# Reading wo inside the attention passes in 8 to 16 KB runs, with a selection product that permutes o and dO

## The chip, the cores and the metric

One core of one Trainium2 chip. The metric is the device time of one execution in microseconds. Runs of one kernel in one job lie 4 to 14 us apart (0.2 to 0.7%), which is as large as the effect that was looked for, so each comparison below is of runs on the same chip in the same job. A ratio is the mean time of one kernel's fast runs over the mean of the other's fast runs of the same rounds, so it is not quite the ratio of the medians that stand beside it. Microseconds given for a ratio are (ratio - 1) x 2029, the median of the kernel before in the first of those jobs.

## The reference, cut to what matters

Two grouped-query attention blocks with a long key/value cache (4 heads of k and v, 65536 positions, 128 wide; 32 query heads; one token) alternate with two dense blocks, and the forward output is returned with all gradients.

```python
q = layernorm(x) @ wq                         # wq 1024 x 4096
o = softmax(q k^T * 128**-0.5) v              # 32 heads of 128
x = x + o.reshape(1, 1, 4096) @ wo            # wo 4096 x 1024
# ... dense block; the whole twice with the same weights; then jax.vjp of all of it
```

wo is used four times: forward in both layers (o times wo), and backward in both (dO = dx times wo transposed). Each group of 8 query heads needs 1024 rows of wo, 2 MB.

## The kernel before

k and v are read four times, in four passes. Between the passes lie stages with the dense blocks. Inside a pass the products with wq and wo run as background jobs, one small step beside each step of the pipeline. All reads go through one queue (SyncE), in order, into a pool of 1 MB granules in SBUF, the arena; two neighbouring granules make a 2 MB read. PE, VectorE and ScalarE follow the program's order. The background jobs share one turn per step of the pipeline: in `step` below, a step of an urgent job uses the turn up, unless it yields "wait"; then an outer product may have it.

```python
def rows_of(W):
    return W.rearrange("(kc p) n -> p kc n", p=P)     # partition p: rows p, 128 + p, ...: runs of one row, 2 KB

def slabs(name, load, nk, kper, ncols, ahead=1, flat=False):
    # ... takes one granule (4 rows of each partition) or, where two neighbours are free, a pair (8 rows)
        nc.sync.dma_start(out=v, in_=load(k, kn))
    # ... yields k, the slab of row k; frees the slot when its rows are used

def wo_slabs(g, ahead=1):
    v = rows_of(A_wo)
    return slabs("s_wo", lambda k, kn: v[:, g * R + k:g * R + k + kn, :], R, 4, 1024, ahead, True)

def g_wo(L, xacc, g, ps=ps_bg, it=None):              # forward: x += o wo
    # ...
    yield from g_mv(it or wo_slabs(g)[0], R, 8, lambda kc: L["oTb"][:, g * R + kc:g * R + kc + 1], ps, fin)

def g_rowdots(slab_it, nk, vcol, nj, finish, name):   # backward: VectorE slab times vector, ScalarE sums
    # ...
    for kc, slab in slab_it:
        if vbc is None:
            vbc = yield from g_bcast_vec(vcol, nj)
        elif kc % 4 == 0:
            for _ in range(WAIT_STEPS):               # 5
                yield "wait"
        t = mvs.tile([P, n], BF, name="mv_t", tag="mv_t", bufs=2)
        nc.vector.tensor_tensor(out=t[:, :], in0=slab, in1=vbc[:, :], op=ALU.mult)
        # ... and `finish` once all rows are done

def g_dO(L, dx, g):
    yield from g_rowdots(wo_slabs(g)[0], R, dx[:], DC, dO_finish(L, g), "%s_dO%d" % (L["name"], g))

class Background:
    def step(self, i):
        # ...
        while self.urgent:                            # products with wq and wo
            r = next(self.urgent[0][1], "end")
            # ... "end": the next job
            if r == "wait":
                break
            return                                    # a step of an urgent job takes the turn of ...
        while self.normal and self.done < self.total * i / self.steps:
            # ... one step of the outer products (weight gradients), and return
```

Pass 4 also makes the gradients of k and v and writes them with those of the weights, 166 MB. Its normal jobs are outer products of rank 2, two matmuls of 128x512 in most of their steps.

Of the kernel before, what the change touches and what calls it, by code (L numbers as in the profile page):

```python
# [10 lines left out]
BF = mybir.dt.bfloat16  # L11
# [9 lines left out]
def kernel(  # L21
# [102 lines left out]
    nc.vector.tensor_reduce(out=M8[:], in_=ident_f[:].rearrange("p (a b) -> p a b", b=16), axis=AX.X, op=ALU.add)  # L124
    M4x = const.tile([P, 4], F32, name="M4x")
    nc.vector.tensor_tensor(out=M4x[:], in0=M8[:, 0:4], in1=M8[:, 4:8], op=ALU.add)


    load = {"act": 0.0, "dve": 0.0, "pe": 0.0}
# [277 lines left out]
    def slabs(name, load, nk, kper, ncols, ahead=1, flat=False):  # L407
        pend = deque()
        ks = deque(range(0, nk, kper))

        def fetch():
            k = ks.popleft()
            i = None
            if ks and flat and NOW["wide"] and not odd_one():
                i = take_pair()
            if i is None:
                kn = min(kper, nk - k)
                sl = Slot(name)
            else:
                kn = min(2 * kper, nk - k)  # L420
                ks.popleft()
                sl = Slot(name, at=i, both=True)
            v = sl.t[:, 0:kn * ncols].rearrange("p (k n) -> p k n", n=ncols)
            nc.sync.dma_start(out=v, in_=load(k, kn))
            pend.append((k, kn, sl, v))

        def gen():
            while ks or pend:
                while ks and len(pend) < ahead:
                    fetch()  # L430
                k, kn, sl, v = pend.popleft()
                for kk in range(kn):
                    yield k + kk, v[:, kk, :]
                sl.free()
        g = gen()
        g_fetch = [fetch for _ in range(ahead)]
        return g, g_fetch
# [12 lines left out]
    def wo_slabs(g, ahead=1):  # L450
        v = rows_of(A_wo)
        return slabs("s_wo", lambda k, kn: v[:, g * R + k:g * R + k + kn, :], R, 4, 1024, ahead, True)

    def w1_slabs(ahead=1):
        v = rows_of(B_w1)
# [375 lines left out]
    def gsl(g):  # L831
        return slice(g * R, (g + 1) * R)
# [10 lines left out]
    def g_wo(L, xacc, g, ps=ps_bg, it=None):  # L843
        def fin(p):
            nc.vector.tensor_tensor(out=xacc[:], in0=xacc[:], in1=p, op=ALU.add)
        yield from g_mv(it or wo_slabs(g)[0], R, 8, lambda kc: L["oTb"][:, g * R + kc:g * R + kc + 1],
                        ps, fin)


    def dO_finish(L, g):  # L850
# [16 lines left out]
        return fin  # L867

    def g_dO(L, dx, g):
        yield from g_rowdots(wo_slabs(g)[0], R, dx[:], DC, dO_finish(L, g), "%s_dO%d" % (L["name"], g))  # L870


    def dn_finish(dn, first):
# [15 lines left out]
    def attn_fwd(p, L, on_group, bg, end=()):  # L889
# [56 lines left out]
        def stats(g, su, S, pm):  # L946
            first = su == first_su[g]
            nm = L["negm"][:, g, su, :]
            v = {}

            def lows():
                pmn = tmp.tile([P, R], F32, name="pmn")
                if SU > HB:
                    pmx = tmp.tile([P, R], F32, name="pmx")
                    nc.vector.tensor_reduce(out=pmx[:], in_=pm[:, :, :], axis=AX.X, op=ALU.max)
                    pin = pmx[:]
                else:
                    pin = pm[:, :, 0]
                if first:
                    nc.vector.tensor_scalar(out=pmn[:], in0=pin, scalar1=-SCALE, scalar2=None, op0=ALU.mult)  # L960
                else:
                    nc.vector.scalar_tensor_tensor(out=pmn[:], in0=pin, scalar=-SCALE, in1=L["negm"][:, g, prev_su[(g, su)], :],
                                                   op0=ALU.mult, op1=ALU.min)
                v["pmn"] = pmn

            def turn():
                v["ptm"] = ps_mv([R, P], F32)
                nc.tensor.transpose(v["ptm"][:, :], v["pmn"][:, :], ident_f[:, :])

            def low():  # L970
                gm = tmp.tile([R, 1], F32, name="gm")
                nc.vector.tensor_reduce(out=gm[:], in_=v["ptm"][:], axis=AX.X, op=ALU.min)
                v["gmb"] = tmp.tile([R, P], F32, name="gmb")
                nc.vector.tensor_scalar(out=v["gmb"][:], in0=ones_f[0:R, :], scalar1=gm[:, 0:1], scalar2=None, op0=ALU.mult)

            def spread():
                v["pnb"] = ps_mv([P, R], F32)
                nc.tensor.matmul(v["pnb"][:, :], lhsT=v["gmb"][:, :], rhs=ident_f[0:R, 0:R], start=True, stop=True)

            def exps():  # L980
                nc.vector.tensor_copy(out=nm, in_=v["pnb"][:])  # L981
                if not first:
                    df = tmp.tile([P, R], F32, name="df")
                    nc.vector.tensor_tensor(out=df[:], in0=nm, in1=L["negm"][:, g, prev_su[(g, su)], :], op=ALU.subtract)
                    al = spool.tile([P, R], F32, name="al", tag="al", bufs=3)
                    nc.scalar.activation(out=al[:], in_=df[:], func=ACTF.Exp)
                    state[("al", g, su)] = al
                v["rs"] = spool.tile([P, R], F32, name="rs", tag="rs", bufs=3)
                state[("rs", g, su)] = v["rs"]
                add_load(act=R * 0.5, dve=1.2)  # L990

            def exp2(h0):
                def f():
                    c0 = su * SU
                    for h in (h0, h0 + 1):
                        nc.scalar.activation(out=E(p, g, c0, SU)[:, :, h], in_=S[:, h, :], func=ACTF.Exp,  # L996
                                             bias=L["negm"][:, g, su, h:h + 1], scale=SCALE, accum_out=v["rs"][:, h:h + 1])
                return f
            for n, fn in ((1, lows), (3, turn), (4, low), (6, spread), (7, exps), (7, exp2(0)), (8, exp2(2)), (9, exp2(4)), (10, exp2(6))):
                after(n, fn)  # L1000
# [168 lines left out]
    def attn_bwd4(p, La, Lb, on_group, bg, stack, end=()):  # L1169
# [16 lines left out]
        def g_setup(g):  # L1186
            sl = gsl(g)
            for i, L in enumerate((La, Lb)):
                nc.vector.tensor_copy(out=DOB[:, g, 0, i * R:(i + 1) * R], in_=L["dOT"][:, sl])
                nc.vector.scalar_tensor_tensor(out=CCf[:, g, 0, i * R:(i + 1) * R], in0=L["qT"][:, sl], scalar=SCALE, in1=L["rZ"][:, sl],  # L1190
                                               op0=ALU.mult, op1=ALU.mult)
                nc.vector.tensor_tensor(out=CCf[:, g, 1, i * R:(i + 1) * R], in0=L["dOT"][:, sl], in1=L["rZ"][:, sl], op=ALU.mult)
            ndt = dspool.tile([64, J, R2], BF, name="ndt4", tag="ndt4", bufs=1)
            for i, L in enumerate((La, Lb)):
                nc.vector.tensor_copy(out=ndt[:, :, i * R:(i + 1) * R], in_=L["nd2"][:, sl].unsqueeze(1).to_broadcast([64, J, R]))
            state["ndt"] = ndt

        def su_setup(g, su):
# [45 lines left out]
        def vS(g, c8):  # L1244
            if c8 == gfirst[g]:
                g_setup(g)
            if c8 == sufirst[(g, c8 // SU)]:
                su_setup(g, c8 // SU)
            if c8 % J == 0:
                state[("xe", g, c8 // J)] = x_transpose(state.pop(("xin", g, c8 // J)))  # L1250
            vt = state.pop(("vt", g, c8))
            for i in range(8):
                s = (c8 + i) % J
                if s == 0:
                    state["ps_dp"] = ps_sc([P, J, R2])
                    nc.tensor.matmul(state["ps_dp"][:, :, :].rearrange("p c r -> p (c r)"), lhsT=sel2[:, :],  # L1256
                                     rhs=state["ndt"][:, :, :].rearrange("o c r -> o (c r)"), start=True, stop=False)
                w = min(4, J - s)
                nc.tensor.matmul(state["ps_dp"][:, s:s + w, :].rearrange("p a b -> p (a b)"), lhsT=vt[:, i, :],  # L1259
                                 rhs=DOB[:, g, 0:w, :].rearrange("p a b -> p (a b)"), start=False, stop=(s == J - 1))  # L1260
            if is_turned("v", g, c8):
                kv_done("v", g, c8)
            if (c8 + 8) % J == 0:
                c0 = c8 + 8 - J
                ps_dp = state["ps_dp"]
                X = dspool.tile([P, J, R2], BF, name="X", tag="X")
                nc.vector.tensor_tensor(out=split2(X[:, :, :]), in0=split2(ps_dp[:, :, :]), in1=E2(g, c0, J), op=ALU.mult)  # L1267
                add_load(dve=0.13 + J * R2 * 0.00105)
                state[("xd", g, c0 // J)] = (X, x_transpose(X[:, :, :]))
                E_done(g, c0, J)  # L1270
# [382 lines left out]
```

## Time and profile before

| | |
|---|---|
| time | 2032.25 us, median of 3 (2031.24 to 2032.61); profiled run 2029.41 us |
| passes 1, 2, 3 | to 376, 423 to 768, 825 to 1174 us |
| pass 4 and its tail | 1235 to 2003, then 24.5 us |
| moved | 795 MB, 392 GB/s over the span |
| reads | 32768 packets of 2 KB, 21248 of 8 KB, 21632 of 16 KB |

The pass limits are the writes of oT, dqT and dOT in the trace. Packets and their times were counted in the trace's table of DMA packets.

From parts 1 and 2 of the page of the kernel before: busy times, then busy tenths of each engine, the DMA engines' share and GB/s in 40 slices of 51 us, and below them the counts of packets.

```profile
PE 1626.9 (80%) x30210; PEld 1332.9 (66%) x30210; DVE 1174.3 (58%) x2358; ACT 1044.6 (52%) x1613; POOL 144.5 (7%) x332
...
DVE  5645455245554543544454457677667777577675
ACT  3434344144344352435363445587667667577675
...
DMA  9999999989999997899999977999999999999996
GB/s 389 420 420 420 419 423 397 371 362 420 420 418 420 420 399 279 352 420 421 420 417 412 401 267 266 370 410 423 422 420 421 393 423 396 363 402 423 421 379 245
DMA packets 110846, 794.98 MB, mean 392 GB/s; under 512 B 9425, under 2 KB 9439, under 8 KB 49375
```

Through passes 1 to 3 the DMA row shows 9 nearly everywhere, mostly at 416 to 423 GB/s, with dips in the dense stages. No compute engine stays at 9. The 49375 packets under 8 KB are mostly 2 KB rows of wq and wo.

The table of stretches for passes 1 to 3 of the kernel before. Columns: stretch and its length, busy us of PE, its weight loads, VectorE, ScalarE and GpSimd (with instruction counts), the granted clock, the DMA share, GB/s.

```profile
core 0: us, PE busy (x) PEld busy (x) DVE busy (x) ACT busy (x) POOL busy (x), PEclk, DMA share, GB/s
20.00:350.00 330.00, 269.22 (x6291) 257.56 (x6289) 181.92 (x392) 141.91 (x335) 0.00 (x0) 0.94 1.00 416
430.00:755.00 325.00, 259.16 (x6161) 247.26 (x6157) 169.56 (x380) 141.41 (x342) 0.00 (x0) 0.94 1.00 415
830.00:1150.00 320.00, 250.96 (x5653) 233.70 (x5650) 153.56 (x288) 142.14 (x194) 0.00 (x0) 0.91 0.99 409
```

The share of 0.99 to 1.00 is the reading to keep: these passes wait for DMA.

In the first of the three stretches one long wait ends, which the view of the wo tensor (who waited for its reads: us, times) and the chain of waits (start, length, what) both show.

```profile
who waited for it (us, times):
  DVE mv_t L549: 16.5, 1
...
DMA to landing us min/median/max: 7.8/18.5/34.8
```

```profile
1711.14 10.81 DMA out_dram<-arena
1722.45 18.47 DMA arena<-in_A_wo_dram
1741.02 0.70 DVE mv_t L549
```

A store frees a slot, the second half of a wo block is read into it in 18.5 us, and VectorE, in program order, waits 16.5 us of that for it.

### The profile page before, as it was taken

To read this page: it belongs to the slowest core of one execution; us is meant where nothing else is said; L and a number is where in the kernel's file an instruction comes from. 1 tells how busy PE (TensorE), PEld (TensorE's weight loads), DVE (VectorE), ACT (ScalarE), POOL (GpSimd) and SP (SyncE) were. 2 spreads that over 40 slices of the span, in tenths; PEclk is the share of its full clock that TensorE was granted. 3 is DMA by queue.
4 is the path that set the end of the run, shared out by engine and by line. 5 is a ranking of instruction groups with operands and counts; after the bars stand their busy time and mean duration, and the time that the engine had idled before them with its cause. 6 is when DMAs were issued, how large, how long until landed. Compare 5 with 4: busy or idle time off the path is not lost. (4 is left out here: it accounts for less than half of the span.)

```text
span 2027.6 us, 67015 instructions
## 1 busy us (share of the span) xinstructions
PE 1626.9 (80%) x30210; PEld 1332.9 (66%) x30210; DVE 1174.3 (58%) x2358; ACT 1044.6 (52%) x1613; POOL 144.5 (7%) x332
## 2 busy tenths in 40 slices
PE   6877888687877877787787887788788888698896
PEld 6877777687777776786676885455455555355554
DVE  5645455245554543544454457677667777577675
ACT  3434344144344352435363445587667667577675
POOL 0000000000000000000000001112121111111111
PEclk9989899799999987898998989889888889798888
DMA  9999999989999997899999977999999999999996
GB/s 389 420 420 420 419 423 397 371 362 420 420 418 420 420 399 279 352 420 421 420 417 412 401 267 266 370 410 423 422 420 421 393 423 396 363 402 423 421 379 245
DMA packets 110846, 794.98 MB, mean 392 GB/s; under 512 B 9425, under 2 KB 9439, under 8 KB 49375
## 3 DMA queue, kind: packets, MB, share of 16 engines
q1 hardware_dynamic: 86510, 624.99, 75.7%
q0 software_dynamic: 24048, 165.70, 19.8%
q8 instruction: 236, 3.87, 0.8%
q14 instruction: 52, 0.42, 0.1%
HBM read 624.96 MB, written 165.69 MB: 390 GB/s over the span
## 5 line engine op out<-in xcount | busy, mean ns | idle before, releaser
L153 DVE COPY kt<-ps_tr 128x1024 bf16<-128x1024 bf16 x724 | 497.8, 689 | 473.8 <-PE ps_tr L913 256.7
L150 ACT CAST arena<-ps_gg 128x1024 bf16<-128x1024 f32 x452 | 439.9, 1009 | 219.0 <-PE ps_gg L1280 160.7
L913 PE MATMUL ps_tr<-ident_b,arena 128*128 128x128 bf16 x3840 | 310.2, 226 | 60.4 <-DMA arena<-in_A_k_cache_dram 45.1
L913 PEld LDWEIGHTS <-arena 128*128 128x128 bf16 x3840 | 234.0, 101 | 66.6 <-DMA arena<-in_A_k_cache_dram 48.1
L153 DVE CAST arena<-ps_gg 128x1024 bf16<-128x1024 f32 (+1 forms) x191 | 228.9, 1198 | 82.4 <-PE ps_gg L1280 48.0
L150 ACT COPY kt<-ps_tr 128x1024 bf16<-128x1024 bf16 x164 | 172.2, 1054 | 183.9 <-PE ps_tr L1105 126.0
L1280 PE MATMUL ps_gg<-GG,xt 64*128 64x512 bf16 x1024 | 211.6, 413 | 46.4 <-DVE arena L153 26.8
L1015 PE MATMUL ps_acc<-arena 128*128 128x64 bf16 (+4 forms) x4096 | 206.0, 196 | 45.7 <-DMA arena<-in_A_v_cache_dram 31.7
L1226 PE MATMUL ps_tr<-ident_b,arena 128*128 128x128 bf16 x1824 | 175.9, 234 | 35.3 <-DMA arena<-in_A_v_cache_dram 34.4
L931 PE MATMUL ps_sc<-L_qpad,kt 128*128 128x64 bf16 (+7 forms) x3584 | 183.4, 194 | 17.9 <-issue 11.5
L996 ACT ACTIVATE arena<-S_sb,L_negm 128x128 bf16<-128x128 f32 x256 | 165.4, 1002 | 57.8 <-DVE L_negm L981 57.7
L1105 PE MATMUL ps_tr<-ident_b,arena 128*128 128x128 bf16 x1920 | 156.3, 228 | 48.3 <-DMA arena<-in_A_v_cache_dram 48.3
L1015 PEld LDWEIGHTS <-arena 128*128 128x128 bf16 x4096 | 159.8, 100 | 50.0 <-DMA arena<-in_A_v_cache_dram 34.8
L1226 PEld LDWEIGHTS <-arena 128*128 128x128 bf16 x1824 | 119.5, 104 | 88.8 <-issue 49.6
L931 PEld LDWEIGHTS <-kt 128*128 128x128 bf16 x3584 | 153.3, 100 | 23.6 <-issue 14.6
L1105 PEld LDWEIGHTS <-arena 128*128 128x128 bf16 x1920 | 118.6, 102 | 52.2 <-DMA arena<-in_A_v_cache_dram 51.0
L1306 PE MATMUL ps_acc<-X,arena 128*128 128x64 bf16 (+3 forms) x2048 | 119.7, 199 | 24.8 <-DMA arena<-in_A_k_cache_dram 24.8
L996 ACT ACTIVATION_READ_ACCUMULATOR arena<-S_sb,L_negm 128x1 f32 x256 | 127.8, 499 | 0.0
L1306 PEld LDWEIGHTS <-arena 128*128 128x128 bf16 x2048 | 87.1, 102 | 59.9 <-issue 33.1
L1150 PE MATMUL ps_acc<-dsT,arena 128*128 128x64 bf16 (+7 forms) x2048 | 103.7, 195 | 20.0 <-DMA arena<-in_A_k_cache_dram 15.8
L1280 PEld LDWEIGHTS <-xt 64*128 64x128 bf16 x1024 | 61.3, 94 | 86.3 <-issue 46.8
L1259 PE MATMUL ps_sc<-DOB,kt 128*128 128x64 bf16 (+3 forms) x1824 | 117.5, 200 | 0.0
(266 smaller groups left out, 2169.3 us busy)
## 6 DMA issues: line engine op xcount, KB each, us to landing
arena<-in_A_k_cache_dram SPq DMA_DIRECT2D x86, 2048.0 KB, 21.5
arena<-in_A_v_cache_dram SPq DMA_DIRECT2D x83, 2048.0 KB, 21.4
out_dram<-arena POOLq DMA_DIRECT2D x151, 1024.0 KB, 11.4
arena<-in_A_v_cache_dram SPq DMA_DIRECT2D x76, 1024.0 KB, 16.5
arena<-in_A_k_cache_dram SPq DMA_DIRECT2D x76, 1024.0 KB, 16.8
arena<-in_B_w_dram SPq DMA_DIRECT2D x32, 896.0 KB, 5.8
arena<-in_A_wq_dram SPq DMA_DIRECT2D x22, 1024.0 KB, 13.8
arena<-in_A_wo_dram SPq DMA_DIRECT2D x18, 1024.0 KB, 17.5
```

The lines of the kernel that those rows point to most:

```text
L150: nc.scalar.copy(out=out, in_=in_)
L153: nc.vector.tensor_copy(out=out, in_=in_)
L913: nc.tensor.transpose(pt[:, i, :], kb8[:, i, :], ident_b[:, :])
L931: nc.tensor.matmul(state["ps_s"][:, s:s + w, :].rearrange("p a b -> p (a b)"), lhsT=kt[:, i, :], rhs=L["qpad"][:, g, 0:w, :].rearrange("p ...
L996: nc.scalar.activation(out=E(p, g, c0, SU)[:, :, h], in_=S[:, h, :], func=ACTF.Exp, bias=L["negm"][:, g, su, h:h + 1], scale=SCALE, accum_ ...
L1015: nc.tensor.matmul(ps_o[:, 0:w, :], lhsT=vb8[:, i, :], rhs=E(p, g, c, w), start=(c % SU == 0), stop=(c % SU == SU - 1), skip_group_check=True)
L1105: nc.tensor.transpose(pt[:, i, :], vb8[:, i, :], ident_b[:, :])
L1150: nc.tensor.matmul(ps_dq[:, 0:w, :].rearrange("p a b -> p (a b)"), lhsT=kb8[:, i, :], rhs=dsT[:, s:s + w, :].rearrange("p a b -> p (a b)") ...
L1226: nc.tensor.transpose(pt[:, i, :], vb8[:, i, :], ident_b[:, :])
L1259: nc.tensor.matmul(state["ps_dp"][:, s:s + w, :].rearrange("p a b -> p (a b)"), lhsT=vt[:, i, :], rhs=DOB[:, g, 0:w, :].rearrange("p a b - ...
L1280: nc.tensor.matmul(pg[:, 512 * h:512 * h + 512], lhsT=xt[64 * h:64 * h + 64, j1 // 8 + m, :], rhs=gg[64 * h:64 * h + 64, :, :].rearrange(" ...
L1306: nc.tensor.matmul(ps_dq[:, 0:w, :].rearrange("p a b -> p (a b)"), lhsT=kb8[:, i, :], rhs=X[:, s:s + w, :].rearrange("p a b -> p (a b)"), ...
```

## The change

Twelve of the sixteen reads of a wo block (those inside the passes) put eight neighbouring rows on one partition, so that a run is 8 KB (one granule, half of the eight rows) or 16 KB (a pair). The rows then lie on other partitions than o and dO do, and small selection products (a matmul with a matrix of zeros and ones) permute those: 3 steps more before the forward read, 3 steps more after the backward one. The intent is fewer, longer DMA packets.

```diff
+    eighth, to_runs, from_runs = ...   # selection constants; the arena starts 928 B further on, all changes taken together
+    def wo_runs(g):
+        v = A_wo[g * 1024:(g + 1) * 1024, :].rearrange("(p k) n -> p k n", k=8)
+        return slabs("s_wo", lambda k, kn: v[:, k:k + kn, :], R, 4, 1024, 1, True)[0]
@@ g_wo
+        each = ...                     # VectorE: oTb times eighth, 128x64
+        yield
+        pt = ps_mv([P, R, 8])
+        nc.tensor.matmul(pt, lhsT=to_runs, rhs=each)
+        yield
+        own, oruns, orunb = ...        # VectorE: mask, sum, cast
+        yield
+        yield from g_mv(wo_runs(g), R, 8, lambda kc: orunb[:, kc:kc + 1], ps, fin)
@@ g_dO
-        yield from g_rowdots(wo_slabs(g)[0], R, dx[:], DC, dO_finish(L, g), ...)
+        def fin(y):
+            each = ...                 # VectorE
+            yield
+            pt = ps_mv([P, R, 8], F32)
+            nc.tensor.matmul(pt, lhsT=from_runs, rhs=each)
+            yield
+            own, back = ...            # VectorE: mask, sum
+            yield
+            yield from dO_finish(L, g)(back[:, :])
+        yield from g_rowdots(wo_runs(g), R, dx[:], DC, fin, ...)
@@ room in SBUF
-  gmb with 2 buffers;  ndt4 [64, 32, 16], copied from nd2 broadcast
+  gmb with 1 buffer;   ndt4 [64, 16], broadcast by the matmul's access pattern
```
(condensed; the arithmetic of the constants and of the masks is left out)

More of the change, by code (lines that the diff above doesn't have):

```diff
@@ L126 @@
     nc.vector.tensor_tensor(out=M4x[:], in0=M8[:, 0:4], in1=M8[:, 4:8], op=ALU.add)
+    eighth = const.tile([P, 8], F32, name="eighth")
+    nc.vector.tensor_reduce(out=eighth[:], in_=ident_f[:].rearrange("p (m e) -> p e m", e=8), axis=AX.X, op=ALU.add)
+    sixt = const.tile([P, 16], F32, name="sixt")
+    nc.vector.tensor_reduce(out=sixt[:], in_=ident_f[:].rearrange("p (m e) -> p m e", e=8), axis=AX.X, op=ALU.add)
+    to_runs = const.tile([P, 8, 16], BF, name="to_runs")
+    nc.vector.tensor_copy(out=to_runs[:, :, :], in_=sixt[:, :].unsqueeze(1).to_broadcast([P, 8, 16]))
+    sixt2 = const.tile([P, 16], F32, name="sixt2")
+    nc.vector.tensor_reduce(out=sixt2[:], in_=ident_f[:].rearrange("p (a m) -> p m a", m=16), axis=AX.X, op=ALU.add)
+    from_runs = const.tile([P, 16, 8], F32, name="from_runs")
+    nc.vector.tensor_copy(out=from_runs[:, :, :], in_=sixt2[:, :].unsqueeze(2).to_broadcast([P, 16, 8]))
     load = {"act": 0.0, "dve": 0.0, "pe": 0.0}
@@ L845, in fin @@
             nc.vector.tensor_tensor(out=xacc[:], in0=xacc[:], in1=p, op=ALU.add)
-        yield from g_mv(it or wo_slabs(g)[0], R, 8, lambda kc: L["oTb"][:, g * R + kc:g * R + kc + 1],
-                        ps, fin)
+        if it is not None:
+            yield from g_mv(it, R, 8, lambda kc: L["oTb"][:, g * R + kc:g * R + kc + 1], ps, fin)
+            return
+        each = tmp.tile([P, R, 8], BF, name="run_each", bufs=1)
+        nc.vector.tensor_tensor(out=each[:, :, :], in0=L["oTb"][:, gsl(g)].unsqueeze(2).to_broadcast([P, R, 8]),
+                                in1=eighth[:, :].unsqueeze(1).to_broadcast([P, R, 8]), op=ALU.mult)
+        yield
+        pt = ps_mv([P, R, 8])
+        nc.tensor.matmul(pt[:, :, :].rearrange("p r k -> p (r k)"), lhsT=to_runs[:, :, :].rearrange("p a b -> p (a b)"),
+                         rhs=each[:, :, :].rearrange("p r k -> p (r k)"), start=True, stop=True)
+        yield
+        own = tmp.tile([P, 8, R], F32, name="run_own", bufs=1)
+        nc.vector.tensor_tensor(out=own[:, :, :], in0=pt[:, :, :].rearrange("p r k -> p k r"),
+                                in1=M8[:, :].unsqueeze(1).to_broadcast([P, 8, R]), op=ALU.mult)
+        oruns = tmp.tile([P, 8], F32, name="run_o")
+        nc.vector.tensor_reduce(out=oruns[:], in_=own[:, :, :], axis=AX.X, op=ALU.add)
+        orunb = tmp.tile([P, 8], BF, name="run_ob")
+        nc.vector.tensor_copy(out=orunb[:], in_=oruns[:])
+        yield
+        yield from g_mv(wo_runs(g), R, 8, lambda kc: orunb[:, kc:kc + 1], ps, fin)
     def dO_finish(L, g):
@@ L869, in g_dO @@
     def g_dO(L, dx, g):
-        yield from g_rowdots(wo_slabs(g)[0], R, dx[:], DC, dO_finish(L, g), "%s_dO%d" % (L["name"], g))
+        def fin(y):
+            each = tmp.tile([P, R, 8], F32, name="run_own", bufs=1)
+            nc.vector.tensor_tensor(out=each[:, :, :], in0=y.unsqueeze(1).to_broadcast([P, R, 8]),
+                                    in1=M8[:, :].unsqueeze(2).to_broadcast([P, R, 8]), op=ALU.mult)
+            yield
+            pt = ps_mv([P, R, 8], F32)
+            nc.tensor.matmul(pt[:, :, :].rearrange("p r k -> p (r k)"), lhsT=from_runs[:, :, :].rearrange("p a b -> p (a b)"),
+                             rhs=each[:, :, :].rearrange("p r k -> p (r k)"), start=True, stop=True)
+            yield
+            own = tmp.tile([P, R, 8], F32, name="run_own", bufs=1)
+            nc.vector.tensor_tensor(out=own[:, :, :], in0=pt[:, :, :], in1=eighth[:, :].unsqueeze(1).to_broadcast([P, R, 8]), op=ALU.mult)
+            back = tmp.tile([P, R], F32, name="run_o")
+            nc.vector.tensor_reduce(out=back[:], in_=own[:, :, :], axis=AX.X, op=ALU.add)
+            yield
+            yield from dO_finish(L, g)(back[:, :])
+        yield from g_rowdots(wo_runs(g), R, dx[:], DC, fin, "%s_dO%d" % (L["name"], g))
     def dn_finish(dn, first):
@@ L972, in low @@
                 nc.vector.tensor_reduce(out=gm[:], in_=v["ptm"][:], axis=AX.X, op=ALU.min)
-                v["gmb"] = tmp.tile([R, P], F32, name="gmb")
+                v["gmb"] = tmp.tile([R, P], F32, name="gmb", bufs=1)
                 nc.vector.tensor_scalar(out=v["gmb"][:], in0=ones_f[0:R, :], scalar1=gm[:, 0:1], scalar2=None, op0=ALU.mult)
@@ L1192, in g_setup @@
                 nc.vector.tensor_tensor(out=CCf[:, g, 1, i * R:(i + 1) * R], in0=L["dOT"][:, sl], in1=L["rZ"][:, sl], op=ALU.mult)
-            ndt = dspool.tile([64, J, R2], BF, name="ndt4", tag="ndt4", bufs=1)
+            ndt = dspool.tile([64, R2], BF, name="ndt4", tag="ndt4")
             for i, L in enumerate((La, Lb)):
-                nc.vector.tensor_copy(out=ndt[:, :, i * R:(i + 1) * R], in_=L["nd2"][:, sl].unsqueeze(1).to_broadcast([64, J, R]))
+                nc.vector.tensor_copy(out=ndt[:, i * R:(i + 1) * R], in_=L["nd2"][:, sl])
             state["ndt"] = ndt
@@ L1256, in vS @@
                     nc.tensor.matmul(state["ps_dp"][:, :, :].rearrange("p c r -> p (c r)"), lhsT=sel2[:, :],
-                                     rhs=state["ndt"][:, :, :].rearrange("o c r -> o (c r)"), start=True, stop=False)
+                                     rhs=state["ndt"][:, :].unsqueeze(1).to_broadcast([64, J, R2]), start=True, stop=False)
                 w = min(4, J - s)
```

## The prediction

> **What bounds the kernel now.** The table of stretches shows four attention passes with dense stages between. In pass 1 (20 to 350 us) the DMA engines are 100% busy at 416 GB/s, in pass 2 (430 to 766) 100% at 414, in pass 3 (827 to 1173) 98% at 406, in pass 4 (1243 to 2002, which also stores 166 MB) about 99% at 401 to 414. No compute engine is that full there: the matmul engine is 78 to 90% busy, VectorE 46 to 75%. So the passes wait for DMA; the list of waits agrees (transposes wait for k and v).
>
> **What the change removes.** 12 of the 16 reads of a 2 MB block of wo (3 per pass) become 8 or 16 KB runs in place of 2 KB runs; the 4 in the dense stages stay. In the trace a read packet of 2048 B takes 87.8 ns on average (median 85), 8192 B 325.6 (309), 16384 B 621.4 (614). The medians fit about 10 ns per packet plus 0.0365 ns per byte. The Trainium skill, "DMA: Bandwidth & Descriptors", section "Why small descriptors are slow (HBM only)", also has a fixed cost per packet; its 3 cycles beside 64 would be 4.5%, this trace shows more. Before: 12288 packets x 87.8 / 16 engines = 67.4 us. After, by the order of issues, five reads of 2 MB (640 packets of 16 KB) and fourteen of 1 MB (1792 of 8 KB): 61.3 us. Saved 6.1 us of saturated DMA. A second estimate, from 2 us stretches: those of nearly only 2 KB packets move 387 GB/s, those without any 419; for 25.2 MB that is 5.0 us.
>
> **What it adds.** Per background wo: three to five small VectorE operations (about 0.2 us each, as the 128x64 cast L838 takes 195 ns) and one small matmul, each a pipeline step apart: about 1 us x 12, over engines with 10% or more to spare, so almost nothing on the path. At the start some reductions and copies on VectorE, about 1 us, under a deep prefetch. In pass 4 the product takes one of two "tr" PSUM buffers, perhaps 1 us each for 3 groups. Removed as well: 8 copies of ndt (208 ns each) in pass 4, off the path.
>
> **What it moves.** Background jobs grow by three steps, so reads of wo and wq are issued a few steps later, and arena slots are paired differently. In pass 4 this reshuffles the outer products and stores. Pass 4's chain of waits holds an 18.5 us read of wo (at 1722 us; VectorE stood 16.5 us for it, in order) and several 20 to 26 us reads of v; which recur is luck, as DMA is full there: plus or minus 8 us.
>
> **Prediction.** Passes 1 to 3 together 4 to 5 us shorter, pass 4 about 1 us shorter with scatter, dense stages unchanged: 2027 us, range 2014 to 2037. Faster by over 2%: 0.02; within 2%: 0.96; slower by over 2%: 0.02.
>
> **What would show it right.** 2048 B read packets fall from 32768 to 20480; passes 1 and 2 shorten by 1.5 us each at slightly higher GB/s; 1 MB wo reads land no later than k and v ones; no new wait over 3 us on the products. **Wrong:** pass times unchanged at lower DMA share (then they weren't DMA-bound), or a wait on the product's PSUM or VectorE in the chain.
>
> **What would make it wrong.** The in-order engines stall on the new steps; the next group's dO comes late in pass 4 and is run at once at the group's start; a worse slot order in pass 4 costing over 10 us; larger read packets taking a larger share from the stores.

(The 4.5% in it is an estimate from that page's figures.)

## More of the kernel before

Now three stretches of pass 4: 20 us around the place where DMA stands idle before the dO of the last group (which is written at 1755.9), the last 60 us of the pass, and the tail after it.

```profile
1735.00:1755.00 20.00, 11.77 (x105) 7.43 (x104) 9.74 (x14) 9.61 (x14) 1.68 (x3) 0.52 0.77 304
1943.00:2003.00 60.00, 55.73 (x715) 35.10 (x713) 44.39 (x72) 42.60 (x47) 10.57 (x18) 0.91 0.93 360
2003.00:2027.60 24.60, 9.94 (x109) 4.41 (x108) 9.88 (x25) 7.70 (x10) 2.51 (x4) 0.65 0.33 129
```

Here the DMA share is below 1: for part of pass 4 DMA stands idle.

## The result, and the profile after

The changed kernel takes 2031.93 us (median of 4, 2030.58 to 2034.32) against 2031.74 of the kernel before in the same runs: ratio 1.001, 95% interval 0.9985 to 1.0034. The forecast was 2027. The gain of 5 us that it named is not in the total.

The page after, its DMA rows and its packets:

```profile
DMA  9999999989999998899999976999999999899985
GB/s 391 421 424 421 423 424 400 379 343 421 424 421 423 425 401 313 360 421 416 419 422 413 391 273 263 356 418 423 419 381 423 394 418 419 332 422 425 424 339 228
DMA packets 101006, 794.98 MB, mean 391 GB/s; under 512 B 9440, under 2 KB 9454, under 8 KB 37102
```

The packets under 8 KB fell by 12273. 2 KB read packets fell from 32768 to 20480, as counted by the prediction. Then the same three stretches of passes 1 to 3:

```profile
20.00:350.00 330.00, 267.81 (x6335) 257.07 (x6335) 185.28 (x411) 142.88 (x336) 0.00 (x0) 0.95 1.00 419
430.00:755.00 325.00, 260.03 (x6173) 247.82 (x6169) 171.59 (x393) 144.05 (x350) 0.00 (x0) 0.95 1.01 419
830.00:1150.00 320.00, 257.88 (x5639) 239.16 (x5636) 154.22 (x296) 141.31 (x192) 0.00 (x0) 0.89 0.99 411
```

Each pass moves 2 to 4 GB/s more. By the landmarks, pass 1 ends at 373.9 in place of 375.6, and pass 4 starts at 1226.1 in place of 1234.8, 8.7 us earlier. Only about half of that lies in the passes: pass 1 is 1.7 us shorter, pass 2 with the dense stage before it 1.6, pass 3 1.3. Another 4.3 lie in the dense stage between passes 2 and 3, 52.1 us in place of 56.4; in the other twelve profiles it takes 51.9 to 55.7 with either kind of read, so this part is scatter. And the three stretches of pass 4, the first again around the idle place before the last dO (which is written at 1766.5 here):

```profile
1735.00:1755.00 20.00, 15.83 (x160) 9.09 (x160) 14.46 (x25) 13.50 (x18) 2.21 (x4) 0.72 0.53 211
1943.00:2003.00 60.00, 56.65 (x689) 35.31 (x687) 44.03 (x83) 42.56 (x47) 10.09 (x17) 0.85 0.79 306
2003.00:2031.20 28.20, 12.79 (x117) 5.72 (x117) 12.28 (x28) 10.43 (x13) 3.24 (x5) 0.61 0.47 184
```

Around the idle place the DMA share fell from 0.77 to 0.53, in the last 60 us from 0.93 to 0.79, and the tail is 28.2 in place of 24.6 us long. The two stretches of 20 us don't lie equally far from the last dO; in the 35 us up to it the share is 0.87 before and 0.74 after. All that was won before pass 4 is given back in it.

VectorE's standstill before the last dO is still there, 14.5 us, and the trace puts it down to the landing of a wo read again. The instruction that it names, X, doesn't read wo, so this is an inference of the profile's from which event came last:

```profile
who waited for it (us, times):
  DVE X L1316: 14.5, 1
...
DMA to landing us min/median/max: 8.8/15.2/32.2
```

The selection product of the backward jobs, by its tile run_own (shortest, median and longest in ns, and who waited for it):

```profile
L906 DVE TENSOR_TENSOR run_own<-L_dO,M x6: 207/220/226, 852.8 to 1756.4; 128x64 f32<-128x64 f32 x6
...
L916 DVE TENSOR_REDUCE run_o<-run_own x6: 219/220/221, 853.9 to 1766.3; 128x8 f32<-128x64 f32 x6
...
L910 PE MATMUL ps_tr<-run_own,from_runs x6: 275/288/303, 1361.9 to 1765.7; 128*128 128x64 f32 x6
...
L914 DVE TENSOR_TENSOR run_own<-ps_tr,eighth x3: 224/225/225, 1362.3 to 1766.0; 128x64 f32<-128x64 f32 x3
...
who waited for it (us, times):
  DVE run_own L914: 1.0, 3
  PEld ps_mv L910: 0.6, 1
  PE ps_mv L910: 0.4, 1
```

Its parts take 0.2 to 0.3 us each, and the waits for this tile are 2 us in all. It is cheap, as predicted.

### The profile page after: what moved, and what is told of

It reads as the page before. It is cut to its first block, busy times and chain, and to the rows that moved or that the text cites. A ratio compares the mean times of both kernels' runs of the same rounds, so it can differ in the third digit from the quotient of the medians.

```text
span 2031.2 us, 67119 instructions
## 1 busy us (share of the span) xinstructions
PE 1646.9 (81%) x30228; PEld 1345.0 (66%) x30228; DVE 1178.5 (58%) x2409; ACT 1043.9 (51%) x1609; POOL 142.2 (7%) x332
## 5 line engine op out<-in xcount | busy, mean ns | idle before, releaser
L164 DVE CAST arena<-ps_gg 128x1024 bf16<-128x1024 f32 (+2 forms) x189 | 224.9, 1190 | 76.6 <-PE ps_gg L1329 35.3
L980 PE MATMUL ps_sc<-L_qpad,kt 128*128 128x64 bf16 (+7 forms) x3584 | 182.6, 194 | 15.2 <-issue 8.3
L980 PEld LDWEIGHTS <-kt 128*128 128x128 bf16 x3584 | 152.3, 100 | 18.7 <-issue 9.0
L1355 PE MATMUL ps_acc<-X,arena 128*128 128x64 bf16 (+3 forms) x2048 | 124.2, 200 | 18.4 <-DMA arena<-in_A_k_cache_dram 18.4
L1199 PE MATMUL ps_acc<-dsT,arena 128*128 128x64 bf16 (+7 forms) x2048 | 105.8, 197 | 17.6 <-DMA arena<-in_A_k_cache_dram 14.5
L1308 PEld LDWEIGHTS <-kt 128*128 128x128 bf16 x1824 | 87.5, 104 | 42.9 <-issue 41.7
## 6 DMA issues: line engine op xcount, KB each, us to landing
arena<-in_A_k_cache_dram SPq DMA_DIRECT2D x76, 1024.0 KB, 14.6
arena<-in_A_wo_dram SPq DMA_DIRECT2D x22, 1024.0 KB, 15.2
```

Source lines behind the costliest of these rows:

```text
L164: nc.vector.tensor_copy(out=out, in_=in_)
L980: nc.tensor.matmul(state["ps_s"][:, s:s + w, :].rearrange("p a b -> p (a b)"), lhsT=kt[:, i, :], rhs=L["qpad"][:, g, 0:w, :].rearrange("p ...
L1199: nc.tensor.matmul(ps_dq[:, 0:w, :].rearrange("p a b -> p (a b)"), lhsT=kb8[:, i, :], rhs=dsT[:, s:s + w, :].rearrange("p a b -> p (a b)") ...
L1308: nc.tensor.matmul(state["ps_dp"][:, s:s + w, :].rearrange("p a b -> p (a b)"), lhsT=vt[:, i, :], rhs=DOB[:, g, 0:w, :].rearrange("p a b - ...
L1355: nc.tensor.matmul(ps_dq[:, 0:w, :].rearrange("p a b -> p (a b)"), lhsT=kb8[:, i, :], rhs=X[:, s:s + w, :].rearrange("p a b -> p (a b)"), ...
```

## The experiments

Two theories at first. A: the three extra steps of each dO job in pass 4 change the order there (turns of the outer products, slots, loads), and that costs what the reads gain. B: pass 4 is paced by compute at the granted clock and takes up any earlier start. The granted clock in pass 4 was indeed lower after (0.855, before 0.885), so B was not idle.

The profiles of all runs, for reference in what follows. "Offset" is where the arena starts in SBUF, over a multiple of 512 B, from the allocation table of the built program. "Body" is pass 4 from its first dO to its last dq. DMA idle was worked out from the packet table in bins of 1 us (1 less the packets' time over 16 engines): in the 35 us before the last dO, and in the last 60 us of the body. Each run has one profile, and in p123, p4, waits and steps6 it is that of the slowest execution, so small differences of bodies say little.

| run | offset B | 16 KB read packet, median ns | start of pass 4 | body | tail | idle before last dO | idle in last 60 |
|---|---|---|---|---|---|---|---|
| before | 288 | 614 | 1234.8 | 768.4 | 24.5 | 5.0 | 4.3 |
| after | 192 | 613 | 1226.1 | 777.2 | 27.9 | 9.4 | 13.2 |
| after_again | 192 | 613 | 1226.9 | 772.5 | 27.7 | 9.8 | 8.8 |
| p123 | 192 | 613 | 1228.5 | 773.9 | 24.6 | 5.0 | 5.5 |
| nosteps | 192 | 613 | 1227.0 | 772.3 | 24.8 | 3.9 | 5.9 |
| waits | 192 | 613 | 1230.6 | 774.4 | 24.6 | 5.0 | 6.1 |
| p4 | 0 | 611 | 1220.1 | 777.2 | 25.9 | 8.6 | 12.8 |
| steps | 288 | 614 | 1231.7 | 777.7 | 26.1 | 10.5 | 11.1 |
| steps6 | 288 | 614 | 1234.8 | 766.6 | 35.6 | 1.7 | 6.4 |
| after_mis | 288 | 614 | 1228.0 | 774.0 | 26.1 | 10.8 | 11.6 |
| after_al | 0 | 611 | 1215.5 | 770.5 | 27.2 | 6.6 | 10.0 |
| before_al | 0 | 611 | 1216.2 | 768.1 | 24.6 | 5.3 | 5.1 |
| before_al2 | 0 | 611 | 1214.2 | 772.0 | 24.4 | 3.4 | 7.2 |
| best | 0 | 611 | 1216.4 | 779.2 | 22.7 | 13.6 | 5.4 |

All outputs are right. The first four below ran on one chip in one job, the next four in another, the last four in a third.

### p123: the change in passes 1 to 3 alone

```diff
     def g_dO(L, dx, g):
+        if L["name"] == "L1":          # pass 4: as before
+            yield from g_rowdots(wo_slabs(g)[0], R, dx[:], DC, dO_finish(L, g), ...)
+            return
```

> The change in passes 1 to 3 alone; pass 4 reads wo as before, and its order of DMA issues is that of the kernel before. Theory A (the three extra steps in pass 4 reshuffle slots, outer products and stores there, which costs what passes 1 to 3 gain): the gain of 8.7 us that the profile shows at the start of pass 4 is kept to the end, 2023 us, ratio 0.996. Theory B (pass 4 is paced by compute at the granted clock, and takes up any earlier start): gain at the start of pass 4 again 8 to 9 us, lost by the end, 2031 us, ratio 1.000.

Measured: 2020.92 us against 2029.09, ratio 0.9967 (0.9951 to 0.9984), 6.7 us faster. The gain is kept: theory A. Its one profiled run was a slow one of its six (2028.79; the others 2018.92 to 2027.98), so its body of 773.9 us says little.

### p4: the change in pass 4 alone

```diff
     def g_dO(L, dx, g):
+        if L["name"] != "L1":          # pass 3: as before; g_wo of passes 1 and 2 likewise
+            yield from g_rowdots(wo_slabs(g)[0], R, dx[:], DC, dO_finish(L, g), ...)
+            return
```

> The change in pass 4 alone; passes 1 to 3 as before. Theory A: pass 4 is 8 to 12 us longer than before's 769 us (1235 to 2003) and its tail 3 us, total 2040 to 2044 us, ratio 1.004 to 1.006. Theory B: pass 4 as long as before, 2031 us or 1 us less, ratio 1.000.

Measured: 2018.94 us, ratio 0.9949 (0.9933 to 0.9965), 10.3 us **faster**. Both theories missed. The profile shows where: pass 4 is as poor as the changed kernel's (body 777.2, idle 8.6 and 12.8), but it starts at 1220.1, 12 to 15 us earlier than in the profiles of the kernel before's passes at its own offset (1231.7 to 1234.8), although passes 1 to 3 read wo in 2 KB rows. Their k and v packets of 16 KB had become faster: median 611 ns in place of 614, with the 10th and the 90th percentile both at 611, from the first microseconds on, before any wo is read. So something outside the reads of wo had changed. With fewer of the change's scratch tiles the arena happened to start on a multiple of 512 B. That is theory C, tried below.

### after_again: the changed kernel once more

> The changed kernel once more, for a narrower interval and a second profile. Both theories: ratio 0.999 to 1.002. Theory A: start of pass 4 8 to 9 us earlier than before, pass 4 with its tail 11 to 13 us longer as in the first profile. Theory B, or scatter of the clock: the start of pass 4 as early, but where in pass 4 the gain is lost differs from the first profile.

Measured: 2029.80 us, ratio 1.0008 (0.9993 to 1.0022). The narrower interval holds: the change is worth nothing in total. The second profile gives the same picture: early start, DMA idle at the same two places.

### steps: the kernel before with three empty steps

```diff
     def g_dO(L, dx, g):
-        yield from g_rowdots(wo_slabs(g)[0], R, dx[:], DC, dO_finish(L, g), ...)
+        def fin(y):
+            if L["name"] == "L1":
+                for _ in range(3):
+                    yield
+            yield from dO_finish(L, g)(y)
+        yield from g_rowdots(wo_slabs(g)[0], R, dx[:], DC, fin, ...)
```

> The kernel before, with three empty steps of the pipeline in pass 4's dO where the changed kernel has its selection product; no product, reads of 2 KB as before. Its order of DMA issues in pass 4 is that of the changed kernel. Theory A: pass 4 alone is 8 to 12 us longer, 2040 to 2044 us, ratio 1.004 to 1.006. Theory B: ratio 1.000. If the product itself costs (a rival within A): ratio 1.000 here and above 1.003 in the run with pass 4 alone.

Measured: 2037.28 us, ratio 1.0042 (1.0030 to 1.0054), 8.5 us slower. No product and no longer read is in it; the empty steps alone cost what the changed kernel loses. Its stretches at the three places of pass 4 (columns as above):

```profile
1739.00:1759.00 20.00, 14.10 (x127) 8.15 (x127) 11.63 (x20) 10.33 (x14) 1.14 (x2) 0.57 0.57 233
1949.00:2009.00 60.00, 55.55 (x704) 35.24 (x702) 44.45 (x84) 43.56 (x48) 10.08 (x17) 0.90 0.82 320
2009.00:2035.50 26.50, 11.18 (x117) 4.96 (x117) 12.04 (x28) 10.43 (x13) 3.24 (x5) 0.69 0.50 195
```

These are like the changed kernel's readings (0.57 and 0.82, where it has 0.53 and 0.79), not like those of the kernel before; so is the share in the 35 us up to the last dO, 0.71.

### before_al: the kernel before with the arena on a multiple of 512 B

```diff
-                v["gmb"] = tmp.tile([R, P], F32, name="gmb")
+                v["gmb"] = tmp.tile([R, P], F32, name="gmb", bufs=1)    # room
+    pad = const.tile([P, 56], F32, name="pad")                           # 224 B
+    nc.gpsimd.memset(pad[:], 0.0)
```

> The kernel before with its arena moved in SBUF to a start that is a multiple of 512 B (288 B over one before; a pad, and one buffer of gmb fewer to make room). No instruction order changes. Theory C (the unexpected gain of the run with pass 4 alone, whose arena lies at a multiple of 512 by accident of its smaller scratch tiles, is the alignment of the arena): the 16 KB read packets fall from a median of 614 ns to 611 and from a mean of 621 to 617, passes 1 to 3 move 424 to 427 GB/s from the first microseconds on, the start of pass 4 is 8 to 13 us earlier than in the kernel before, ratio 0.990 to 0.994. If the layout doesn't matter: packets 614, ratio 1.000.

Measured: 2009.20 us against 2028.75, ratio 0.9899 (0.9882 to 0.9917), 20.5 us faster with the same order of DMA issues. Its stretches of passes 1 to 3:

```profile
20.00:350.00 330.00, 269.04 (x6400) 257.12 (x6398) 184.06 (x403) 143.35 (x340) 0.00 (x0) 0.96 1.01 423
430.00:755.00 325.00, 261.15 (x6206) 249.35 (x6203) 170.10 (x381) 146.52 (x352) 0.00 (x0) 0.94 1.01 422
830.00:1150.00 320.00, 254.20 (x5672) 236.77 (x5668) 152.33 (x287) 139.88 (x190) 0.00 (x0) 0.91 1.01 421
```

416, 415 and 409 GB/s became 423, 422 and 421. Byte for byte the 2 KB packets gained most: 2 us stretches filled with them (some 14 in each profile) move about 400 GB/s here, where they moved 387 in the kernel before; stretches without any, about 424 in place of 419. In sum the 16 KB packets gave more: up to the start of pass 4 the packets' time over 16 engines falls by 16 us, of which 8 are theirs and 5 the 2 KB packets'. The smaller gmb isn't the cause: the changed kernel has it too, and with the arena 288 B off (after_mis) its packets take 614 ns.

### after_al: the changed kernel with the arena on a multiple of 512 B

```diff
+    pad = const.tile([P, 16], F32, name="pad")       # and bc_rows with one buffer, for room
```

> The changed kernel with its arena at a multiple of 512 B (192 B over one as it stands). Theory C: packets of 611 ns, and the total falls by the same 10 to 16 us: ratio to before 0.991 to 0.995, and 0.998 to 1.003 of the aligned kernel before, as without alignment. If the layout doesn't matter: 1.001.

Measured: 2013.46 us, ratio 0.9922 (0.9899 to 0.9946), 15.8 us faster than before. Theory C holds for both kernels. At equal alignment the change is again no gain.

### nosteps: the product of pass 4 in no steps of its own

```diff
             each = ...
-            yield
+            if L["name"] != "L1":
+                yield
```
(at all three of g_dO's new steps)

> The changed kernel with the selection product of pass 4 in no steps of its own (its instructions come within the last step of the job), so that pass 4's order of DMA issues is that of the kernel before; reads and product as changed, arena as in the changed kernel. Theory A (the order in pass 4 costs 8 us): ratio 0.995 to 0.997, as with passes 1 to 3 alone or 1 us better, 2020 us. If the product or the larger read packets cost something in pass 4: 1.000.

Measured: 2023.23 us, ratio 0.9965 (0.9946 to 0.9984), 7.1 us faster. It has the product and the longer reads in all four passes, and the order of the kernel before in pass 4. So neither the product nor the length of packets costs anything in pass 4: the steps do.

### after_mis: the changed kernel with the arena 288 B off, as before

```diff
+    pad = const.tile([P, 24], F32, name="pad")
```

> The changed kernel with its arena 288 B over a multiple of 512, as in the kernel before (192 as it stands). It tells how much of the change's gain in passes 1 to 3 is a by-product of its new constants moving the arena. Theory C with a part for the change: packets 614 instead of 613 ns, total 1 to 3 us longer, ratio 1.001 to 1.003. If all of the gain in passes 1 to 3 came from the reads: 1.001.

Measured: 2036.22 us, ratio 1.0026 (1.0007 to 1.0045), 5.3 us slower than before. The changed kernel as it stands had 1.0008 (0.9993 to 1.0022) in another job; the intervals overlap, so a part of its gain may come from its arena lying 192 and not 288 B off. In the profiles the end of pass 1 is reproducible to 0.3 us: 375.4 to 375.6 (three profiles of 2 KB reads, 288 B off), 374.7 (long reads, 288), 373.9 to 374.2 (five of long reads, 192), 369.6 to 369.9 (five at a multiple of 512, with either kind of read). By these, with one profile for the middle step, the 1.5 us that pass 1 gains are about half the reads' and half the offset's. Pass 3, from its first dO to its last dq, tells the reads apart better: 349.2 to 349.4 us with 2 KB reads at 288 B, 347.5 with long reads at 288, 347.5 to 348.0 with long reads at 192. There the gain is the reads'. On an aligned arena no gain of the reads is left to be seen in either pass (pass 3 takes 344.0 to 344.6 us with 2 KB reads, 343.9 to 344.8 with long ones), though the packet times before pass 4 still sum to some 3 us less over 16 engines (at 288 B: 7 us less). Why is open.

### waits: the product's steps give their turn away

For this job theory A was sharpened to A2: it is the turns that count. A step of an urgent job takes the turn of a step of the outer products, and three steps in each of three groups are nine turns.

```diff
             each = ...
-            yield
+            yield "wait" if L["name"] == "L1" else None
```

> The changed kernel with one word more: in pass 4 the three steps of the selection product let the outer products of the weight gradients have their turn in the same step. Theory A2 (what the extra steps cost in pass 4 is turns: 9 turns, 18 outer-product matmuls, move from the first three groups into the last group and the tail, where loads are done and DMA stands idle): the matmuls by group are before's 60, 54, 52, 58, 16 again (the changed kernel: 56, 48, 44, 74, 18), DMA idle in pass 4 falls from 39 to 46 us to 27 to 34, ratio 0.995 to 0.998 as with the product in no steps. If the three steps cost by their waits on PSUM or by their order of loads: 1.001.

Measured: 2023.06 us against 2030.66, ratio 0.9968 (0.9950 to 0.9986), 6.5 us faster, though the product keeps its steps. The outer-product matmuls of the groups of pass 4 and the tail, counted in the trace, are 60, 54, 52, 58 and 16 as in the kernel before; the changed kernel has 56, 48, 44, 74 and 18. Its stretches:

```profile
1740.00:1760.00 20.00, 14.32 (x154) 8.89 (x154) 13.22 (x20) 13.04 (x18) 2.39 (x5) 0.69 0.77 307
1945.00:2005.00 60.00, 54.73 (x715) 34.94 (x713) 44.52 (x73) 42.83 (x47) 10.57 (x18) 0.94 0.90 352
2005.00:2029.60 24.60, 10.09 (x109) 4.41 (x108) 9.74 (x24) 7.54 (x10) 2.51 (x4) 0.64 0.33 129
```

0.77 and 0.90, and a tail of 24.6 us: the kernel before again (in the 35 us up to the last dO, 0.86), although this profile is of the slowest of the six runs (2031.36 us; the others 2020.48 to 2026.42). The order of its reads in pass 4 isn't quite that of the kernel before, so that exact order isn't needed for it. One word in three lines brings back what was lost.

### steps6: six empty steps

```diff
-                for _ in range(3):
+                for _ in range(6):
```
(the run called steps)

> The kernel before with six empty steps in pass 4's dO in place of three (which gave ratio 1.0042). Theory A2: twice the turns are lost, 16 matmuls more fall into the tail after the last group (32 in place of 18), so another 8 to 12 us: ratio 1.008 to 1.011. If the cost was luck of slots: anything from 0.999 to 1.006, not in line with the number of steps.

Measured: 2034.41 us, ratio 1.0016 (1.0002 to 1.0029), 3.2 us slower. Theory A2 as stated fails: twice the steps cost less than half. One part of it holds. The tail has 32 outer-product matmuls and is 35.6 us long, 11 more than before. But the body is the shortest of all, 766.6 us, and the idle time before the last dO is gone:

```profile
1740.00:1760.00 20.00, 18.38 (x237) 12.20 (x238) 17.09 (x39) 14.98 (x22) 3.30 (x6) 0.84 0.92 349
1941.00:2001.00 60.00, 55.54 (x690) 34.86 (x688) 46.72 (x87) 43.65 (x48) 9.45 (x16) 0.89 0.90 362
2001.00:2036.90 35.90, 17.51 (x147) 6.55 (x146) 18.08 (x40) 14.88 (x18) 4.68 (x7) 0.61 0.51 198
```

### best: aligned, with more turns given away

The arena of after_al, with "wait" in the product's three steps and in two of dO_finish, so that the outer products have six turns more than in the kernel before.

> The changed kernel with its arena at a multiple of 512 B, with the product's steps and the two of dO's finish giving up their turns in pass 4. Six turns more than the kernel before has in the first half of pass 4 (120 of 240 matmuls there; before 112, changed 104). Theories A2 and C together: 20 us by alignment, 2 to 3 us by the reads in passes 1 to 3, 0 to 4 us by the turns: 2003 to 2008 us, ratio 0.987 to 0.990, at least as fast as the aligned kernel before in the same job. If the reads are worth nothing: as the aligned kernel before.

Measured: 2020.03 us, ratio 0.9944 (0.9926 to 0.9961). It missed by 12 us and more: slower than the aligned kernel before. The tail is the shortest (22.7 us) and the body the longest (779.2), with 13.6 us of DMA idle before the last dO. More turns for the outer products early on are not better either.

### before_al2: the aligned kernel before, again

> The aligned kernel before once more, on the chip of the run called best, and for a second profile: ratio 0.988 to 0.992, start of pass 4 at 1214 to 1220 us, packets of 611 ns.

Measured: 2013.10 us, ratio 0.9914 (0.9898 to 0.9930), and the start of pass 4 at 1214.2. The gain of alignment is repeated on another job, 17 to 20 us. This is the fastest kernel that ran; it isn't the change, but a pad of 224 B in the kernel before.

## Why the prediction was right or wrong, point by point

- **The total.** 2031.93 us lies in the range of 2014 to 2037, and "within 2%" was right. The centre, 5 us below the kernel before, was not: the effect is 0 to 2 us the other way. A range of 23 us takes in any outcome that was in question here, so that the total fell in it is no evidence for the account.
- **Passes 1 to 3, "together 4 to 5 us shorter".** Five profiles of the changed passes start pass 4 at 1226.1 to 1230.6 us, three of the kernel before's at 1231.7 to 1234.8: 6 us in the mean, of which 4 lie in the passes (pass 2 taken with the dense stage before it) and 2 in a dense stage that scatters by itself. The kernels without the new order in pass 4 (p123, nosteps, waits) are 6.5 to 7.1 us faster. The sign and the size hold; the reason only in part. Some of the gain of pass 1 is the arena's new offset, and on an aligned arena a gain of the reads in passes 1 and 3 can't be seen, so that the reads won as much as forecast was partly luck of where the arena lay. The two estimates of 5.0 and 6.1 us rested on 2 KB packets at 387 GB/s, and that figure contained the misalignment.
- **Pass 4, "about 1 us shorter with scatter".** This is the step that failed. Pass 4 with its tail takes 800.2 and 805.1 us in two profiles, 792.8 before: 7 to 12 us longer. Over all profiles the six with the changed kernel's order take 797.8 to 805.1 us (mean 801.7), the six with the outer products' turns of the kernel before 792.7 to 799.0 (mean 796.1): 6 us. The prediction named "a worse slot order in pass 4" as a way to be wrong, but counted it as luck of plus or minus 8 us. It is no luck from run to run: the order is fixed when the program is built. Six profiles with the changed kernel's order have 8.8 to 13.2 us of idle DMA in the last 60 us, six with the outer products' turns of the kernel before (five of them with exactly its order of reads) 4.3 to 7.2; before the last dO it is 6.6 to 10.8 against 3.4 to 5.3. Empty steps alone (1.0042) bring the loss, and the product without turns of its own (0.9968, 0.9965) takes it away.
- **"DMA is full there", of pass 4.** Wrong in its premise. It was read from stretches of 200 to 260 us with a DMA share of 0.99 to 1.01; in bins of 1 us the body of the kernel before has some 28 us of idle DMA, and that of the changed kernel 40 to 44. The body has places where DMA stands idle, as in the kernel before while VectorE stands 16.5 us for a wo block in program order, and in the last 60 us. In such places fewer DMA microseconds buy nothing.
- **What the change adds.** Right: 0.2 to 0.3 us an operation, waits of 2 us in all for run_own, no wait over 3 us.
- **1 MB wo reads "land no later than k and v ones".** Nearly: 15.2 us in the median against 14.6 and 15.0, before 17.5 against 16.8 and 16.5.
- **Theory B** (the clock) falls as the whole cause: the empty steps lose 8.5 us at a mean granted clock of 0.900, where the kernel before had 0.901 in the same job, and p4 gains 10.3 us at 0.8995. (The profile of p123, with 0.868 in pass 4, doesn't speak against B, since it is of the one run in six that kept the least of the gain.) But the clock has a part in the scatter: among the runs of one kernel, 0.01 less of it goes with some 5 us more (103 runs). Taken at equal clock, the empty steps still cost about 8 us, and p123, nosteps and waits, whose mean clock is 0.005 to 0.007 higher than that of the kernel before, still gain 3 to 5 of their 6 to 7 us (estimates from that slope and the list of runs). How much of their gain came by way of the clock isn't settled.
- **What stays open.** Why the body answers to the order as it does: one count of turns does not explain it (in one profile each the body changes by +9 us for three steps, -2 us for six, and +7 to +11 us for six turns the other way, on an aligned arena; bodies with the turns of the kernel before differ by 6 us among themselves). Which of the two idle places makes how much of the loss wasn't tried apart. Why packets into a start 288 B off take longer, no run shows. The smaller ndt4 was never tried alone. And the product with "wait" on an aligned arena, without the turns of dO_finish, was not run; whether it beats the aligned kernel before is not known.

## What to carry to other kernels

When fixed-turn background jobs share one slot per pipeline step, an extra step costs a turn of some other job, whatever the step itself takes; run the empty step alone, and see whether small steps should give their turn away. What a lost turn costs has to be measured: six empty steps cost less here than three. A stage whose DMA share averages 0.99 can still hold idle stretches; look at it in bins of 1 us. Before costing a change by a packet's time, look where the destination starts: here a pad of 224 B was worth some four times what the change aimed at. And when one part of a change gives a result that both theories miss, compare stretches that the change cannot have touched.

## What the Trainium skill lacked or had wrong

- "SBUF — State Buffer", section "Operand start alignment", says of its measurements that they are about legality and timed nothing; no page gives the speed of a DMA by where its SBUF side starts. Here a start 288 B over a multiple of 512 gave 416, 415 and 409 GB/s in passes 1 to 3 and 614 ns for a 16 KB read packet, a multiple of 512 gave 423, 422 and 421 GB/s and 611 ns, and 17 to 20 us of 2029. An offset of 192 B gave 613 ns; with the long reads it moved 419, 419 and 411 GB/s, against 418, 418 and 410 at 288 B and 423, 424 and 421 at a multiple of 512. The pad moves the tiles behind it as well; that it is the arena's start that counts rests on the packets into the arena. Which power of two is enough was not tried.
- "DMA: Bandwidth & Descriptors", section "How a descriptor splits into AXI transactions", gives extra beats to a descriptor that doesn't start at a multiple of 256 B, but doesn't say whether this holds for the SBUF side of a long load, or what it costs in time; the numbers are those above.
- The same page, section "Why small descriptors are slow (HBM only)": its 3 cycles per packet would be 4.5% of the time of 2 KB (an estimate from that page). With the arena aligned the medians of 84 ns for 2 KB and 611 ns for 16 KB give 8.7 ns per packet plus 0.0368 ns per byte, so 10% for 2 KB by packet time (an estimate from those medians), and stretches of 2 KB packets move about 400 GB/s where others move about 424, 6%.
